# Sums of the u half moved to GpSimd, scores of five tiles in four quarters of the array, and a new order of steps

## The chip, the cores and the metric

The program runs on one core of a Trainium2 chip. A core has TensorE (PE, with its weight loads as PEld), VectorE (DVE), ScalarE (ACT), GpSimd (POOL) and SyncE (SP), which issues all transfers here. Each engine takes its instructions strictly in the order in which the program lists them, and waits on semaphores. The metric is device microseconds of one execution; the median of three runs is compared.

## The reference, cut to what matters

```python
def _attn_ref(q, k, v):            # 8 batches, 8 heads, 576 tokens, head_dim 64
    q_c, k_c, v_c = (a.reshape(B, H, 9, 64, 64) for a in (q, k, v))   # chunks of 64 tokens
    scores = np.matmul(q_c, k_c.transpose(0, 1, 2, 4, 3)) / np.sqrt(D)
    attn = softmax(scores)          # with 1e-9 added to the sum
    return np.matmul(attn, v_c).reshape(B, H, S, D)

def _moe_ref(x, w_in, g_ln, w_sg, b_sg, w_out):   # x: (8, 576, 512)
    h = gelu_tanh(x @ w_in)                       # w_in: 512 x 1024
    u, v = h[..., :512], h[..., 512:]
    v_n = layer_norm(v) * g_ln                    # eps 1e-6
    v_s = einsum('ts,bsd->btd', w_sg, v_n) + b_sg[None, :, None]
    return x + (u * v_s) @ w_out
```

The host hands w_in and w_out over as pairs of 32-bit words of double precision numbers; the kernel makes a high and a low part of each value of them.

## The kernel before

**Tiling.** The 4608 tokens are 36 tiles of 128. A step is named by a letter and a number. For tile t, A loads q, k, v, S makes scores and softmax (L484, L505), T the transposed weights (L544), O the product with v and the split of x into a high part xh, a low part xl and the plain xf (L571, L607). Tiles from 5 on that come in pairs have P and Q in the place of S and O. For batch b, v is the v half (v_unit, L645: product, gelu, layer norm), u the u half (u_unit, L696, or by seven partial products, q), s the product over tokens (L721) and o or p the output product.

**Weights.** W and w make the high and low words of w_in's v half in four pieces, X and x those of its u half (L278 to L283). The begin step loads nothing; it works on a landed piece: ACT takes the absolute value of the upper word (L186), DVE rebuilds the float f and two half-width remainders p and q (L188 to L233). The end step (pair_end, L235) lets ACT write the high word hi = -f, rounded, and lets TensorE add four terms in PSUM, f by a float32 identity, q and p by two bfloat16 multiples of the identity, and hi by the rounded identity (L246). ACT copies the sum out as the low word (L248).

**Partial products.** From batch 2 on the u half and the output product use sums of quarters of the weights, a scheme with seven products in the place of eight. The sums of w_in's quarters are the steps E0 to E3 (sum_product, L360): TensorE adds 4, 2, 2 and 4 quarters by identities in PSUM (L370), ACT and DVE split the sum into high and low (L375 to L380), and SP stores it to DRAM, from where a ring of four buffers is filled later (begin_ring, L384). The sums for w_out are made on GpSimd already (sum_step, L321 to L334). The steps Y turn w_out into high and low words, in eight pieces (o_w, L285).

**Scores.** An array of 128 by 128 can be used as four quarters of 64 by 64. From tile 5 on, each head and chunk is placed by the function half (L456) so that all four quarters occur (L502). Tiles 0 to 4 use only the two quarters on the diagonal, rows 0 to 63 with columns 0 to 63, and rows 64 to 127 with columns 64 to 127 (L493).

**Order.** The order of work is written out by hand: ORDER (L53 to L108) is a string of 1641 step names, and each occurrence runs the named step's generator up to its next yield. Every engine's queue is this order. In PSUM, three two-bank buffers (pm) go round among the products, and two banks (banks) serve the attention.

## Time and profile before

| what | value |
|---|---|
| median of 3 runs | 502.53 us (502.31 to 502.89) |
| profiled execution | 501.2 us |
| its span | 499.4 us |
| TensorE busy | 480.9 us, 96% of the span |
| VectorE, ScalarE, GpSimd busy | 393.1, 339.0, 118.4 us |
| mean granted TensorE clock | 1.00 |

The span runs from the first to the last instruction of the core; 1.8 us of the profiled execution lie around it, and the execution is 1.3 us below the median of the runs. Busy time of TensorE comes from matmul records with modelled ends, so the pace of a series is read from one start to the next, not from the mean duration. A releaser behind an arrow names what ended an engine's idle time. Times of a stretch are microseconds from the span's start.

### The profile page before, as it was taken

The numbers are of one execution on the slowest core, as the hardware profiler recorded it, in microseconds if no ns is written. First come the engines' busy times: TensorE is split into PE (matmuls) and PEld (weight loads), VectorE is DVE, ScalarE is ACT, GpSimd is POOL, SyncE is SP. The second block draws the span as 40 slices with busy tenths as digits, with TensorE's granted clock in tenths as the row PEclk, the third lists the DMA queues.
The fourth block names the chain that finished last, engine by engine and source line by source line (L and its number), as shares of the span: only waits on it lengthen the run. The fifth ranks groups of instructions, "written<-read, shape, count | busy, mean of one in ns | idle before, by whom it ended". The sixth has DMA issues, their size and how long they took to land.

```text
span 499.4 us, 12551 instructions
## 1 busy us (share of the span) xinstructions
PE 480.9 (96%) x5107; PEld 440.6 (88%) x5112; DVE 393.1 (79%) x678; ACT 339.0 (68%) x643; POOL 118.4 (24%) x106
## 2 busy tenths in 40 slices
PE   4899999999999999999999999999999999999996
PEld 2567799889999899997999889997999889998996
DVE  8887969896844797878859788778959788868666
ACT  5787898844655779849894588638885597724420
POOL 0112100010291432116210261114320271105200
PEclk9999999999999999999999999999999999999999
DMA  7976301269276883887887938297876936093616
GB/s 290 368 206 201 111 22 45 86 169 310 74 217 231 281 265 112 226 282 198 270 216 209 298 106 276 62 296 228 250 211 201 297 112 210 6 308 116 226 41 214
DMA packets 70189, 97.98 MB, mean 196 GB/s; under 512 B 36978, under 2 KB 50290, under 8 KB 70132
## 3 DMA queue, kind: packets, MB, share of 16 engines
q1 hardware_dynamic: 70132, 97.18, 62.5%
q8 instruction: 40, 0.66, 0.6%
q14 instruction: 17, 0.14, 0.1%
HBM read 80.38 MB, written 16.78 MB: 195 GB/s over the span
## 4 chain that ended last, share of the span: by engine, by line
PE 79%; ACT 8%; DVE 8%; DMA 3%; issue 1%; SPq 0%; ACTq 0%; DVEq 0%
PE pm L731 23%; PE pm L654 14%; PE pm L852 12%; PE pm L784 11%; PE pm L910 5%; PE pm L703 5%; PE banks L502 3%; PE pm L601 3%; DMA wsg<-w_in 2%; ACT ptT L566 2%; PE pm L246 2%; ACT hs L658 1%; DMA qkv_t<-qkv 1%; ACT L658 1%; DVE blocks L556 1%
## 5 line engine op out<-in xcount | busy, mean ns | idle before, releaser
L731 PE MATMUL pm<-wsg,v 128*128 128x288 f32 x768 | 108.1, 296 | 0.7 <-DVE u L796 0.7
L731 PEld LDWEIGHTS pm<-wsg,v 128*128 128x128 f32 x768 | 103.8, 189 | 1.5 <-DVE u L796 1.0
L667 POOL TENSOR_TENSOR sm<-sm,neg_half 128x1 f32<-128x1 f32 x36 | 28.4, 791 | 126.2 <-DVE sm L665 120.0
L539 POOL TENSOR_TENSOR pt<-pt,den 128x1024 f32<-128x1024 f32 (+1 forms) x15 | 26.4, 1760 | 131.8 <-DVE den L536 123.9
L654 PE MATMUL pm<-wv_h,xl 128*128 128x512 f32 x128 | 51.8, 404 | 2.4 <-ACT xf L633 1.3
L566 ACT COPY ptT<-blocks 32x256 f32<-32x256 f32 x124 | 50.1, 404 | 2.3
L654 PE MATMUL pm<-wv_h,xh 128*128 128x512 f32 x128 | 50.6, 395 | 0.0
L654 PE MATMUL pm<-wv_l,xh 128*128 128x512 f32 x128 | 50.6, 395 | 0.0
L784 PE MATMUL pm<-xt,ring 128*128 128x288 f32 x288 | 42.8, 297 | 0.0
L852 PE MATMUL pm<-gh,ring 128*128 128x288 f32 x192 | 40.9, 297 | 0.0
L784 PEld LDWEIGHTS pm<-xt,ring 128*128 128x128 f32 x288 | 39.5, 188 | 0.8
L662 DVE BATCH_NORM_STATS2 sm<-hs 128x6 f32<-128x512 f32 x36 | 24.8, 688 | 19.3 <-ACT hs L658 19.2
L737 DVE TENSOR_TENSOR u<-pm,u 128x576 f32<-128x576 f32 x24 | 18.0, 752 | 19.2 <-PE pm L731 17.1
L784 PE MATMUL pm<-xh,ring 128*128 128x288 f32 x144 | 32.0, 298 | 0.3 <-ACT hs L658 0.3
L654 PEld LDWEIGHTS pm<-wv_h,xl 128*128 128x128 f32 x128 | 24.0, 188 | 8.8 <-ACT xf L633 2.2
L852 PEld LDWEIGHTS pm<-gh,ring 128*128 128x128 f32 x192 | 31.5, 188 | 0.3
L852 PE MATMUL pm<-tv,ring 128*128 128x288 f32 x216 | 31.7, 296 | 0.0
L675 ACT ACTIVATE v<-hs,sm 128x512 fp32r<-128x512 f32 x32 | 22.9, 721 | 12.3 <-DVE hs L669 12.1
L852 PEld LDWEIGHTS pm<-tv,ring 128*128 128x128 f32 x216 | 29.9, 188 | 0.6
L669 DVE SCALAR_TENSOR_TENSOR hs<-hs,sm,g_bc 128x512 f32<-128x512 f32 x36 | 29.6, 828 | 0.0
L654 PEld LDWEIGHTS pm<-wv_h,xh 128*128 128x128 f32 x128 | 24.0, 188 | 5.8
L852 PE MATMUL pm<-gl,ring 128*128 128x288 f32 x96 | 28.3, 295 | 0.0
(175 smaller groups left out, 1144.9 us busy)
## 6 DMA issues: line engine op xcount, KB each, us to landing
ring<-factors SPq DMA_DIRECT2D x84, 512.0 KB, 4.3
qkv_t<-qkv SPq DMA_DIRECT2D x32, 512.0 KB, 5.0
qkv_t<-qkv SPq DMA_DIRECT2D x124, 64.0 KB, 4.0
out_dram<-u SPq DMA_DIRECT2D x18, 288.0 KB, 5.3
factors<-fac SPq DMA_DIRECT2D x16, 256.0 KB, 2.8
out_dram<-ot SPq DMA_DIRECT2D x14, 288.0 KB, 2.1
qkv_t<-qkv SPq DMA_DIRECT2D x3, 768.0 KB, 11.7
wsg<-w_in SPq DMA_DIRECT2D x4, 512.0 KB, 4.1
```

The lines of the kernel that those rows point to most:

```text
L539: eng.tensor_tensor(pt, pt, den.unsqueeze(2).broadcast_to([P, n, D]), op=ALU.mult)
L566: nc.scalar.copy(ptT[q[1 - a], :, a, :], blocks[q[a], :, 1 - a, :])
L654: nc.tensor.matmul(pv, a[:, kt, tok], c[:, kt, :], start=(i == 0), stop=(i == 11))
L662: nc.vector.bn_stats(st, h)
L667: nc.gpsimd.tensor_tensor(rs, rs, neg_half, op=ALU.pow)
L669: nc.vector.scalar_tensor_tensor(h, h, mv[:, 0:1], g_bc, op0=ALU.subtract, op1=ALU.mult)
L675: nc.scalar.mul(hi, h, rs)
L703: nc.tensor.matmul(pm[:, j, :HS], a[:, kt, dc], c[:, kt, j * HS : (j + 1) * HS], start=(i == 0), stop=(i == 11))
L731: nc.tensor.matmul(pm[:, j, :HS], a[:, dc], c[:, m, j * HS : (j + 1) * HS], start=(i == 0), stop=(i == len(ops) - 1))
L784: nc.tensor.matmul(pm[:, e, :HS], a[:, k, e * P : (e + 1) * P], c[:, k, :], start=starts and i == 0, stop=i == len(ops) - 1, skip_group_ch ...
L852: nc.tensor.matmul(pm[:, e, :HS], a[:, k, e * P : (e + 1) * P], c[:, k, :], start=starts and i == 0, stop=i == len(ops) - 1, skip_group_ch ...
L910: nc.tensor.matmul(pm[:, j, :HS], a[:, kt, ec], c[:, kt, j * HS : (j + 1) * HS], start=(i == 0), stop=(i == len(ops) - 1),)
```

## The change

Four things change. In the end step of the four u pieces, GpSimd adds f and hi into a bfloat16 remainder d, and TensorE adds three bfloat16 terms in the place of four. The quarter sums E0 to E3 are ten GpSimd additions in the order of sum_inner, in a buffer that shares its place with w_out's high words, in the place of twelve matmuls; ACT and DVE split the sums from SBUF, not from PSUM. The first five tiles' scores lie in four quarters and two PSUM banks, with the softmax and the product with v indexed to match. ORDER is written anew; of its 61 lines one stands below.

```diff
@@ -51,61 +51,61 @@
 ORDER = """
-L0 L1 A0 L2 M0 L3 A1 W0 A2 A3 W0 A4 W0 W1 W0 W1 w0 W0 W1 W0 W1 S0 W1 w1 W1 W2 w0 S0 W2 S0
...
+L0 L1 A0 L3 M0 L2 A1 W0 A2 A3 W0 A4 W0 W1 W0 W1 w0 W0 W1 W0 W1 S0 W1 w1 W1 W3 w0 S0 W3 S0
...
@@ -116,6 +116,7 @@
 X_LOW_ON = {5: "vector", 6: "vector", 7: "vector", 4: "vector"}
 U_KEPT_ON_ACT = (1, 5, 6)
 RING = 4
+REST_ON_POOL = {"u": (0, 1, 2, 3), "v": ()}
 
 
 ON_POOL = ("l0", "l1")
@@ -232,15 +233,21 @@
         yield
         nc.vector.scalar_tensor_tensor(q, lw, 9, top, op0=ALU.logical_shift_right, op1=ALU.bitwise_or)
 
-    def pair_end(n, hi, lo, st):
+    def pair_end(n, hi, lo, st, rest=False):
 
         f = st[:, 2 * n : 3 * n].bitcast(F32)
         p, q = st[:, 3 * n : 4 * n].bitcast(BF16)[:, 1::2], st[:, : 2 * n].bitcast(BF16)[:, :n]
         shape = lambda a: a.rearrange("p (k c) -> p k c", k=hi.shape[1]) if len(hi.shape) == 3 else a
         nc.scalar.mul(hi, shape(f), -1.0)
         yield
+        if rest:
+
+            d = st[:, : 2 * n].bitcast(BF16)[:, n : 2 * n]
+            nc.gpsimd.tensor_tensor(shape(d), shape(f), hi.bitcast(F32), op=ALU.add)
+            yield
         ps = ps_m.tile([P, 2, 512], F32, name="pm")[:, 0, :n]
-        terms = [(ident, f), (low[0], q), (low[1], p), (ident_r, hi)]
+        ones = ident_r.bitcast(BF16)[:, 1::2]
+        terms = [(low[0], q), (low[1], p), (ones, d)] if rest else [(ident, f), (low[0], q), (low[1], p), (ident_r, hi)]
         for i, (a, c) in enumerate(terms):
             out_ps = shape(ps) if c is hi else ps
             nc.tensor.matmul(out_ps, a, c, start=(i == 0), stop=(i == len(terms) - 1))
@@ -261,7 +268,7 @@
         yield from pair_begin(DH, staged["v", kt])
 
     def v_w_end(kt):
-        yield from pair_end(DH, wv_h[:, kt, :], wv_l[:, kt, :], staged["v", kt])
+        yield from pair_end(DH, wv_h[:, kt, :], wv_l[:, kt, :], staged["v", kt], kt in REST_ON_POOL["v"])
         yield
         u_w_load(kt)
 
@@ -280,7 +287,7 @@
 
     def u_w_end(dt):
         cols = slice(dt * P, (dt + 1) * P)
-        yield from pair_end(DH, wu_h[:, :, cols], wu_l[:, :, cols], staged["u", dt])
+        yield from pair_end(DH, wu_h[:, :, cols], wu_l[:, :, cols], staged["u", dt], dt in REST_ON_POOL["u"])
 
     def o_w(et, half):
         nonlocal wout_h, wout_l
@@ -353,31 +360,28 @@
         yield
         keep_factor("o", p, (hi, lo))
 
-    def begin_sums():
-        held["neg"] = const.tile([P, P], F32R, name="neg", tag="low")
-        nc.scalar.mul(held["neg"], ident, -1.0)
-
-    def sum_product(n):
-
-
-        h11, l11, h12, l12, h21, l21, h22, l22 = quarters("u")
-        if n in (0, 3):
-            held["sum"] = ps_m.tile([P, 2, 512], F32, name="pm")
-        ps = held["sum"][:, 0].rearrange("p (k e) -> p k e", k=2)
-        pos, neg = (((h21, l21, h22, l22), ()), ((), (h11, l11)), ((), (h12, l12)), ((h11, l11), (h21, l21)))[n]
-        terms = [(ident_r, a) for a in pos] + [(held["neg"], a) for a in neg]
-        for i, (a, c) in enumerate(terms):
-            nc.tensor.matmul(
-                ps, a, c, start=n in (0, 3) and i == 0, stop=i == len(terms) - 1, skip_group_check=n in (1, 2)
-            )
-        yield
+    def sum_inner(n):
+
+
+        if n == 0:
+            t = w_out_tile(0, F32)
+            held["sums"] = [t[:, i * 4 * P : (i + 1) * 4 * P].rearrange("p (k e) -> p k e", k=2) for i in range(3)]
+        h11, l11, h12, l12, h21, l21, h22, l22 = (a.bitcast(F32) for a in quarters("u"))
+        a, c, d = held["sums"]
+        steps = (
+            ((a, h21, h22, ALU.add), (c, l21, l22, ALU.add), (a, a, c, ALU.add)),
+            ((a, a, h11, ALU.subtract), (a, a, l11, ALU.subtract)),
+            ((d, h12, a, ALU.subtract), (d, d, l12, ALU.add)),
+            ((c, h11, h21, ALU.subtract), (d, l11, l21, ALU.subtract), (c, c, d, ALU.add)),
+        )[n]
+        for k, (o, x, y, op) in enumerate(steps):
+            nc.gpsimd.tensor_tensor(o, x, y, op=op)
+            yield
+        src = steps[-1][0]
         hi, lo = factor_tiles()
-        nc.scalar.mul(hi, ps, -1.0 if n == 2 else 1.0)
-        yield
-        if n == 2:
-            nc.vector.scalar_tensor_tensor(lo, ps, -1.0, hi.bitcast(F32), op0=ALU.mult, op1=ALU.subtract)
-        else:
-            nc.vector.tensor_tensor(lo, ps, hi.bitcast(F32), op=ALU.subtract)
+        nc.scalar.copy(hi, src)
+        yield
+        nc.vector.tensor_tensor(lo, src, hi.bitcast(F32), op=ALU.subtract)
         yield
         keep_factor("u", (5, 6, 3, 7)[n], (hi, lo))
 
@@ -457,7 +461,7 @@
 
 
         m = t % NINE
-        j = (h + (c if m == 4 else (m - (m > 4)) % 2)) % 2
+        j = (h + (c if m == 4 or t < PE_TILES else (m - (m > 4)) % 2)) % 2
         return slice(j * D, (j + 1) * D)
 
     def att_load(t):
@@ -486,11 +490,12 @@
         if tiles[0] < PE_TILES:
             for t in tiles:
                 qt = state[t]
-                sc = ps_m.tile([P, 2, H, D], F32, name="pm")[:, 0]
+                pm = ps_m.tile([P, 2, 512], F32, name="pm")
+                sc = pm[:, :, : HP * D].rearrange("p j (hp s) -> p j hp s", hp=HP)
                 for h in range(H):
                     for c in range(2):
-                        r = slice(c * D, (c + 1) * D)
-                        nc.tensor.matmul(sc[r, h, :], qt[r, 0, h, :], qt[r, 1, h, :], start=True, stop=True)
+                        r, o = slice(c * D, (c + 1) * D), half(t, h, c)
+                        nc.tensor.matmul(sc[o, h % 2, h // 2, :], qt[r, 0, h, :], qt[r, 1, h, :], start=True, stop=True)
                 yield from softmax((t,), sc)
             return
         for i, t in enumerate(tiles):
@@ -510,8 +515,9 @@
         pt = att.tile([P, (2 if big else 1) * H, D], F32, name="pt", tag="pt2" if big else "pt1", bufs=1)[:, :n]
         nmax = small.tile([P, 2 * H], F32, name="nmax", bufs=2)[:, :n]
         den = small.tile([P, 2 * H], F32, name="den", bufs=1)[:, :n]
-        rows = (lambda a: a) if t < PE_TILES else (lambda a: a.rearrange("p (c k) s -> p c k s", c=2))
-        cols = (lambda a: a) if t < PE_TILES else (lambda a: a.rearrange("p (c k) -> p c k", c=2))
+        order = "(k c)" if t < PE_TILES else "(c k)"
+        rows = lambda a: a.rearrange(f"p {order} s -> p c k s", c=2)
+        cols = lambda a: a.rearrange(f"p {order} -> p c k", c=2)
         yield
         nc.vector.tensor_reduce(cols(nmax), sc, axis=AX.X, op=ALU.max, negate=True)
         scale = 1.0 / math.sqrt(D)
@@ -522,7 +528,7 @@
             yield
             for h in range(H):
                 col = slice(h, h + 1)
-                src = sc[:, h, :] if t < PE_TILES else sc[:, h // HP, h % HP, :]
+                src = sc[:, h % 2, h // 2, :] if t < PE_TILES else sc[:, h // HP, h % HP, :]
                 nc.scalar.activation(pt[:, h, :], src, AF.Exp, bias=nmax[:, col], scale=scale, accum_out=den[:, col])
         else:
             yield
@@ -578,10 +584,9 @@
             for hp in range(HP):
                 for c in range(2):
                     for j in range(2):
-                        r = slice(j * D, (j + 1) * D)
+                        r, q = slice(j * D, (j + 1) * D), half(t, j, c)
                         nc.tensor.matmul(
-                            xo[r, hp, c * D : (c + 1) * D], vt[r, c, hp, :], ptT[r, hp, c * D : (c + 1) * D],
-                            start=True, stop=True,
+                            xo[r, hp, c * D : (c + 1) * D], vt[r, c, hp, :], ptT[r, hp, q], start=True, stop=True
                         )
             yield from keep(t, xo.rearrange("p hp (c s) -> p c hp s", c=2))
             return
@@ -936,7 +941,7 @@
         "Y": lambda k: o_w(k // 2, k % 2), "R": lambda k: begin_ring(), "f": lambda k: load_factor(),
     }
     steps.update({
-        "B": sum_step, "C": split_sum, "K": lambda k: keep_quarters("o"), "N": lambda k: begin_sums(), "E": sum_product,
+        "B": sum_step, "C": split_sum, "K": lambda k: keep_quarters("o"), "E": sum_inner,
         "k": lambda k: keep_quarters("u"),
     })
```

The order of the engines shows this at three places. First TensorE around the first v_unit (v00): `pm<-wv_h,xl` is its first matmul, `wsg_189` is the first u piece, `banks<-ptT,qkv_t` an O step and `banks<-ident,pt` a T step. Before:

```order
L493 MATMUL pm<-qkv_t 64x64 x16
L246 MATMUL pm<-wsg_189,ident 128x512
L246 LDWEIGHTS low
L246 MATMUL pm<-wsg_189,low 128x512
L246 LDWEIGHTS low
L246 MATMUL pm<-wsg_189,low 128x512
L246 MATMUL pm<-wu,ident 128x512
L582 MATMUL banks<-ptT,qkv_t 64x64 x16
L549 MATMUL banks<-ident,pt 128x128 x4
L654 MATMUL pm<-wv_h,xl 128x512
```

After, from the last matmuls of that v_unit on:

```order
L659 MATMUL pm<-wv_l,xh 128x512
L659 MATMUL pm<-wv_h,xh 128x512
L253 LDWEIGHTS low
L253 MATMUL pm<-wsg_189,low 128x512
L253 LDWEIGHTS low
L253 MATMUL pm<-wsg_189,low 128x512
L253 LDWEIGHTS ident
L253 MATMUL pm<-wsg_189,ident 128x512
L588 MATMUL banks<-ptT,qkv_u 64x64 x16
L555 MATMUL banks<-ident,pt 128x128 x4
```

The end of the first u piece stood two steps ahead of v00 and now stands right behind it, with three bfloat16 matmuls in the place of four terms, and ahead of tile 3's O step, whose data lie in `qkv_u`.

Second GpSimd from its first tile work on: `xl<-xf,xh` is the low part of x of tiles 0 and 1, `sm<-sm,neg_half` the layer norm's inverse root, `sums` the w_out sums, `wu` w_in's u half. Before:

```order
L626 TENSOR_TENSOR xl<-xf,xh 128x2x4x64 x2
L414 MEMSET wsg_550 64x576
L667 TENSOR_TENSOR sm<-sm,neg_half 128x1 x9
L539 TENSOR_TENSOR pt<-pt,den 128x1024 x2
L334 TENSOR_TENSOR sums<-wout_981 128x512
```

After (`wsg_189` to `wout_439` are the four u pieces, `wout_667` the buffer of the sums):

```order
L631 TENSOR_TENSOR xl<-xf,xh 128x2x4x64
L246 TENSOR_TENSOR wsg_189<-wsg_189,wu 128x512
L631 TENSOR_TENSOR xl<-xf,xh 128x2x4x64
L246 TENSOR_TENSOR wsg_203<-wsg_203,wu 128x512
L672 TENSOR_TENSOR sm<-sm,neg_half 128x1
L246 TENSOR_TENSOR wout_314<-wout_314,wu 128x512
L418 MEMSET wsg_604 64x576
L672 TENSOR_TENSOR sm<-sm,neg_half 128x1
L378 TENSOR_TENSOR wout_667<-wu 128x512
L246 TENSOR_TENSOR wout_439<-wout_439,wu 128x512
```

The pieces' additions and the sums of E0 now stand between the low parts of x and the inverse roots, where nothing stood.

Third ScalarE ahead of the Q step of tiles 7 and 8, in the s units of batch 0: `pt<-pt` is the exponential of those tiles, `ptT<-blocks` their transposed weights, `st` a piece of w_out, `gh<-gt` the gated value. Before:

```order
L531 ACTIVATE pt<-pt 128x1024
L199 ACTIVATE st<-st 128x256
L186 ACTIVATE st<-st 128x256
L747 CAST gh<-gt 128x576
L199 ACTIVATE st<-st 128x256
L633 COPY xf<-pm 128x2x4x128
L186 ACTIVATE st<-st 128x256
L560 COPY ptT<-blocks 128x512
L566 COPY ptT<-blocks 32x8x32 x4
```

After:

```order
L537 ACTIVATE pt<-pt 128x1024
L382 CAST fac<-wout_667 128x512
L638 COPY xf<-pm 128x2x4x128
L382 CAST fac<-wout_667 128x512
L200 ACTIVATE st<-st 128x256
L187 ACTIVATE st<-st 128x256
L752 CAST gh<-gt 128x576
L200 ACTIVATE st<-st 128x256
L187 ACTIVATE st<-st 128x256
L566 COPY ptT<-blocks 128x512
L572 COPY ptT<-blocks 32x8x32 x4
```

Two copies of quarter sums (`fac<-wout_667`) stand ahead of the transposed weights, and the high word of a w_out piece has gone behind them.

## Rows read from the trace of the kernel before

**Rows 1.** The page, part 1: engines' busy us, share of span, instructions.
```profile
PE 480.9 (96%) x5107; PEld 440.6 (88%) x5112; DVE 393.1 (79%) x678; ACT 339.0 (68%) x643; POOL 118.4 (24%) x106
```

**Rows 2.** Windows: stretch, length, then PE, PEld, DVE, ACT, POOL busy; clock; DMA.
```profile
30.00:90.00 60.00, 58.19 (x650) 50.31 (x652) 50.52 (x95) 51.72 (x106) 6.65 (x7) 1.00 0.36 109
40.00:120.00 80.00, 80.00 (x805) 72.15 (x806) 68.13 (x146) 61.60 (x113) 7.62 (x10) 1.00 0.43 125
70.00:80.00 10.00, 10.00 (x188) 9.77 (x188) 8.14 (x12) 9.83 (x16) 0.00 (x0) 1.00 0.20 54
80.00:90.00 10.00, 10.00 (x128) 9.58 (x127) 9.90 (x23) 8.49 (x19) 0.00 (x0) 1.00 0.09 28
110.00:120.00 10.00, 10.00 (x129) 9.64 (x128) 6.87 (x12) 4.63 (x7) 0.55 (x1) 1.00 0.96 265
180.00:200.00 20.00, 19.27 (x254) 18.57 (x253) 17.16 (x25) 19.27 (x30) 6.03 (x5) 1.00 0.47 157
```

**Rows 3.** Chain that ended last, in order of time: start, us, what.
```profile
12.06 10.83 DMA wsg<-w_in
...
70.65 1.09 PE banks L502 x64
...
109.86 0.92 PE pm L370 x4
```

**Rows 4.** Timeline of PE: start, us, line, tiles, count, idle before it.
```profile
14.54 1.15 PE L493 MATMUL pm<-qkv_t 64*64 64x64 f32 x32 [0.61 <-DMA qkv_t<-qkv]
...
32.66 0.48 PE L654 MATMUL pm<-wv_h,xl 128*128 128x512 f32 x1
...
36.84 0.66 PE L549 MATMUL banks<-ident,pt 128*128 128x128 f32 x4 [1.14 <-DVE xl L631]
38.17 1.15 PE L582 MATMUL banks<-ptT,qkv_u 64*64 64x64 f32 x32 [0.68 <-ACT xf L633]
```

**Rows 5.** Timeline of PE, the end steps of the last two u pieces.
```profile
54.92 1.12 PE L246 MATMUL pm<-wout,ident 128*128 128x512 f32 x2
55.88 0.38 PE L246 MATMUL pm<-wout,low 128*128 128x512 bf16 x1
56.13 0.59 PE L246 MATMUL pm<-wu,ident 128*128 128x512 f32 x1
56.56 1.02 PE L246 MATMUL pm<-wout,ident 128*128 128x512 f32 x2
```

**Rows 6.** Timelines of POOL and DVE around the low parts of x.
```profile
19.82 1.27 POOL L626 TENSOR_TENSOR xl<-xf,xh 128x512 fp32r<-128x512 f32 x1 [18.53 <-ACT xh L624]
30.68 1.29 POOL L626 TENSOR_TENSOR xl<-xf,xh 128x512 fp32r<-128x512 f32 x1 [9.59 <-ACT xh L624]
...
19.96 1.69 DVE L539 TENSOR_TENSOR pt<-pt,den 128x512 f32<-128x512 f32 x1
...
22.28 0.17 DVE L521 TENSOR_SCALAR nmax<-nmax 128x8 f32<-128x8 f32 x1
...
26.43 0.69 DVE L539 TENSOR_TENSOR pt<-pt,den 128x512 f32<-128x512 f32 x1
...
30.76 1.25 DVE L521 TENSOR_SCALAR nmax<-nmax 128x8 f32<-128x8 f32 x1
```

**Rows 7.** Groups by line, shapes apart: POOL's sums, DVE's subtractions and ACT's copies beside them.
```profile
L334 POOL TENSOR_TENSOR sums<-wout 128x512 f32<-128x512 f32 x4 | 5.6, 1418 | 0.0
...
L352 DVE TENSOR_TENSOR fac<-sums,fac 128x512 fp32r<-128x512 f32 x4 | 2.7, 687 | 0.7 <-DMA out_dram<-ot 0.6
...
L350 ACT CAST fac<-sums 128x512 fp32r<-128x512 f32 x4 | 2.4, 622 | 0.3 <-DVE den L536 0.2
```

**Rows 8.** Timelines of ACT and PE where tiles 7 and 8 meet.
```profile
84.92 1.65 ACT L566 COPY ptT<-blocks 32x256 f32<-32x256 f32 x4
...
87.71 1.16 PE L601 MATMUL pm<-ptT,qkv_t 64*64 64x64 f32 x64
```

More of the change, by code (lines that the diff above doesn't have):

```diff
@@ new lines @@
+W3 S0 W3 W3 w1 W3 w0 w0 S0 W2 S0 w3 W2 T0 W2 w1 w1 W2 S1 T0 W2 w2 O0 S1 W2 S2 A5 O0 S1 w2
+O0 S2 S1 O0 S2 O0 S1 S3 w2 w2 S1 O0 D8 S1 X0 S3 S2 X0 T1 X0 X0 S4 S3 T1 X0 S2 S3 O1 S2 x0
+X0 T2 A6 O1 S3 x0 X1 w3 S4 T2 S3 O1 S3 O2 X2 O1 S4 X1 w3 w3 T3 A7 O2 v00 X2 S4 O2 X2 X1 X2
+X1 T3 x0 X2 O2 S4 x1 X2 O3 S4 G0 X1 T4 X1 v00 O3 v01 v00 x1 X3 O3 x2 v00 X3 O3 v00 v00 T4 X3 x2
+x0 O4 X3 v01 x1 v00 A8 v02 O4 g0 v01 x1 x3 O4 v00 O4 O4 O4 x2 v01 O4 X3 O4 v01 P5 v01 O4 v02 X3 E0
+v01 u00 v02 x2 v01 g0 x3 v02 g2 P5 g4 v02 v03 g3 g2 g1 g4 v02 g4 g1 g0 x3 v02 g4 v03 x3 v02 v04 k0 P5
@@ new lines @@
+E0 g3 P5 E0 v03 u01 P5 E3 v03 u00 P5 v04 P5 v03 E0 v03 u02 u01 T5 v03 v04 T5 v03 T5 v04 T5 T6 T5 v04 P7
+T5 v04 T6 T6 u03 P7 T6 T6 T6 u02 P7 v04 E0 v04 Q5 v04 v04 E0 E1 v04 v04 s00 Y0 Q5 Y1 E1 u03 Q5 E2 P7
+s01 s00 E2 E1 P7 Q5 E2 E1 P7 Y0 E1 Y0 P7 s00 s02 Y1 Y0 s00 Y1 Y0 T8 Y0 T8 Y1 Y0 Y1 T8 Y0 T8 Y1
+s03 T8 Y0 T8 T7 E2 T7 s02 E2 E3 T7 T7 Y1 T7 T7 E3 s02 s01 Q7 s02 s01 v10 Y1 Y2 Q7 s03 Y3 Y1 s03 Q7
+E3 E3 Q7 v11 s01 E3 Y0 s03 Y2 Y2 Y0 Y1 Y2 Y4 Y2 Y1 v12 Y2 Y5 Y2 v10 Y2 Y3 v10 Y3 v11 Y2 Y3 Y2 v10
@@ new lines @@
+v13 Y3 v12 v10 Y2 Y4 Y3 Y6 v10 Y4 Y5 Y4 Y5 Y3 Y4 v10 Y3 Y4 o00 Y3 Y4 Y3 Y5 Y4 Y5 Y6 Y4 Y6 Y5 Y4
+Y3 v13 Y6 Y7 Y4 Y5 A9 u10 Y6 Y5 Y6 v10 Y6 Y5 Y6 Y5 v11 Y7 Y6 Y7 u11 Y5 u10 Y7 A10 v13 Y6 Y7 Y6 Y7
+v13 Y7 v13 v13 A11 u12 Y7 u11 v12 v13 Y7 v13 Y7 v11 v12 v11 Y7 v11 u13 A12 u12 v12 v12 v11 o00 v12 v11 K0 v12 P9
+u13 s10 P9 o00 P9 P9 s11 P9 s10 P9 s10 P9 s10 P11 s12 T9 P11 T9 T9 s11 T9 T9 T10 T9 s11 P11 T10 s13 s11 T10
+P11 s12 T10 P11 T10 T10 s12 P11 Q9 s13 P11 s12 s13 o01 A13 B0 T12 s13 T12 A14 B1 T12 o02 T12 o01 T12 T11 T12 B5 T11
```

94 lines of the change are left out of this document (39 added, 55 removed).

## The prediction

> **What bounds the kernel now.** I read the page's first part first: TensorE is busy for 96% of the span, VectorE for 79%, ScalarE for 68%, GpSimd for 24% [rows 1]. An average hides stages, so I read the windows next. From 40 to 120 us TensorE shows 80.00 of 80 us, at a granted clock of 1.00 [rows 2]: there, each microsecond of matmul taken out is worth a microsecond, provided that the other engines can follow. Whether they can is the second thing to see in these rows. From 30 to 90 us VectorE works 50.52 of 60 us and ScalarE 51.72 [rows 2]. They have 9.5 and 8.3 us of idle time left; by 110 to 120 us ScalarE is down to 4.63 of 10. Third the chain of work and the timeline of the start. Until about 23 us ScalarE's queue waits for the first piece of w_in's u half: that transfer ends at 12.06 + 10.83 = 22.89 us [rows 3]. The first v_unit begins at 32.66 us, and TensorE then idles twice more, 1.14 and 0.68 us [rows 4].
>
> **The quarter sums** leave TensorE as twelve matmuls. Four of them take 0.92 us on the chain [rows 3], so 0.23 each, and twelve take 2.76 us, all at places where TensorE was never idle. I count 2.76 us in full. ScalarE's copy and VectorE's subtraction for each sum remain, but three of the four now come ahead of the s units' end instead of behind 110 us.
>
> **The low words of the u pieces.** One end step lasts from 54.92 to 56.56, 1.64 us; one bfloat16 matmul in it from 55.88 to 56.13, 0.25 us [rows 5]. Three of these make 0.75 us, so each piece saves 0.89 us of TensorE, and the last three pieces, which lie where TensorE is full, 2.67 us. The first piece moves from ahead of the first v_unit to behind it: 0.75 us enters the full stretch and 1.64 us leaves the start.
>
> **The scores in four quarters.** A tile in two quarters takes 1.15 us [rows 4]; a pair of later tiles in four takes 1.09 [rows 3], so 0.55 for one. Five tiles save 5 x 0.6 = 3.0 us, but all of them ahead of 32.66 us, where TensorE waits for others. I give this no term of its own. The whole that leaves TensorE is 2.76 + 4 x 0.89 + 3.0 = 9.3 us, and that is the upper bound of the gain without new overlap.
>
> **The start.** The same bytes are ordered ahead of the u pieces, so I keep ScalarE's start at about 22.9 us. Behind it the first v_unit needs tile 1's low part, which GpSimd ended at 30.68 + 1.29 = 31.97 us [rows 6], and a free TensorE, which came at 32.66 [rows 4]. The change puts one of two absolute values (0.6 us) behind tile 1's parts and takes 1.64 us out of TensorE's queue ahead of the v_unit. Following both queues piece by piece I get tile 1's low part at about 31.0 and the v_unit at about 31.3, a gain of 1.4 (bounds 0.7, TensorE's own delay alone, and 2.4, if the transfers come a microsecond earlier too). Of the two idle times of 1.82 us behind it the first piece's 0.75 us of work fills a part, and I leave 0.7 us idle, ahead of tile 4's output, whose transposed weights stand behind a table load and other work on ScalarE. That gives 1.4 + (1.82 - 0.7) - 0.75 = 1.8 us.
>
> **Sum without contention:** 2.76 + 2.67 + 1.8 = 7.2 us.
>
> **What is added.** GpSimd gets fourteen additions on tiles of 128x512. Such sums last 1.29 to 1.42 us [rows 6, 7], so 18 to 20 us of GpSimd, in a stretch where it now works 6.65 of 60 us [rows 2]. Its own time is hidden: the quarter sums are not needed until batch 2. What is not hidden is VectorE. While GpSimd made the low part of x at 19.82, VectorE's normalisation of tile 1 took 1.69 us, not the 0.69 of tile 2's; while it made that of tile 1, at 30.68, a tiny scaling took 1.25 us, not 0.17 [rows 6]. So an addition can cost VectorE up to 1.08 us, fourteen up to 15 us. At the other end, VectorE's subtractions beside the w_out sums kept their 687 ns, and it was GpSimd that lasted 1.42 in place of 1.29 [rows 7]; that is a price of nought. No price is below nought, since the removed work was on TensorE and VectorE does the same subtractions. I take 4 us of VectorE time in all, nearer to nought, because half of VectorE's work there reads PSUM or is a reduction. The Trainium skill, page SBUF — State Buffer, section "Who interferes with whom", has a rule that speaks against this change: GpSimd and a VectorE operation with two SBUF inputs exclude each other for a whole instruction. By it all fourteen would block somebody, and if always VectorE, the sum would be a loss; the rows above agree that a wait occurs and show both sides bearing it.
>
> **Whether the cover holds.** The test is the Q step of tiles 7 and 8, which TensorE reaches at 87.71 us; ScalarE ends the transposed weights for it at 84.92 + 1.65 = 86.57 [rows 8]. To come 1.8 + 2.67 = 4.5 us earlier, both helpers must give up idle time. ScalarE has 8.3 us less 1.9 for three early copies of 0.62 [rows 7]; VectorE 9.5 us less 1.4 for two early subtractions of 0.69 [rows 7], less 1.4 that I allow for w_out work moved ahead, less the 4 us above: 2.7 us, plus the 1.1 us that TensorE's weights were early (87.71 less 86.57). That falls short of 4.5 by about 0.6 us, which I take off. In VectorE's queue the waiting subtraction of a quarter sum holds back the softmax and transposes of tiles 7 and 8, and TensorE waits for those. Behind this point ScalarE has room (4.63 of 10 us), and from 180 to 200 us, where ScalarE works 19.27 of 20 us and TensorE 19.27 [rows 2], the last sum's splitting is gone, so I expect neither gain nor loss.
>
> **Forecast:** 7.2 - 0.6 = 6.6 us less. The profiled execution of 501.2 us would become 494.6 and its span 492.8; the median of the runs, 1.3 us above it, goes from 502.5 to **495.9 us**. A difference of about 0.2%, 1 us, is what a measurement here can tell from none.
>
> **The rivals.**
> 1. ScalarE and VectorE cannot follow at all up to the Q step, and only what lies behind it is won: 2.76 us, 499.8 us; with half of the 4.5 us, 497.5. For it: 9.90 and 9.83 of 10 us in the windows before 90 us [rows 2]. Against it: the idle time exists, and the order was written for shorter TensorE steps. Chance of 497.3 to 500.5: 0.22.
> 2. All that is taken out comes through, 9.3 us: 493.2 us. For it: the start is shortened by the scores too, and 0.7 us of idle time left above may vanish. Against it: the transfer that ends at 22.89 us. Chance of 492 to 494.5: 0.15.
> 3. GpSimd's additions make VectorE the bound and the kernel slower. Place: VectorE's queue between the first v_unit and the Q step of tiles 7 and 8. If every addition costs 1.08 us, VectorE loses 15 us, 11 more than counted, and the sum turns to 502.5 - 6.6 + 11 = 507 us. It decides for slower from 10.6 us on, 0.76 us for each of the fourteen. Against it: rows 7, where GpSimd bore the wait. Chance 0.06.
> 4. The change does not do what it says, because TensorE's gain is given back at 180 to 200 us, where ScalarE is full: 502 us, no change. Against it: ScalarE has half its time free from 110 us on and arrives there earlier as well. Chance 0.05.
> The forecast's own case, 494.5 to 497.3, has the rest, 0.52.
>
> **How the numbers follow.** The range leaves out the slower and the unchanged case, 0.11, and some hundredths at either end: 493.0 to 500.0. Faster by over 0.2% is 0.52 + 0.22 + 0.15 = 0.89, within 0.2% is 0.05, slower 0.06.
>
> **What would show it.** The quarter sums' matmuls are gone and u pieces' end steps take about 0.75 us; the first v_unit starts near 31.3 us; the Q step of tiles 7 and 8 near 83.8 us, and with no idle time of TensorE over 1 us in front of it; GpSimd's busy time rises from 118 to about 137 us; VectorE's two-input operations of 0.69 us show up at 1.2 to 1.9 beside GpSimd's additions, with about 4 us more in sum. The forecast is wrong if TensorE idles for microseconds between 40 and 90 us behind VectorE or ScalarE, or if the order opens new waits behind 180 us, where I have followed only the order of TensorE.

## The result, and the profile after

The changed kernel takes 495.75 us (median of six runs, 493.63 to 497.74), the kernel before 501.51 on the same chips (six runs, 499.44 to 502.89). The ratio is 0.9886 with a 95% interval of 0.9849 to 0.9923. The forecast was 495.9, in a range of 493.0 to 500.0. The profiled execution went from 501.2 to 493.63 us, its span from 499.4 to 491.8.

Executions of the changed kernel differ in TensorE's mean granted clock, from 1.00 down to 0.991, and the time goes with it (493.63 and 494.42 us at 1.00; 495.34 to 497.74 at 0.997 and below); the profile shown here is one at 1.00, and so is that of before.

The page's first part and the windows after, to be held against [rows 1] and [rows 2]:

```profile
PE 473.1 (96%) x5087; PEld 434.3 (88%) x5092; DVE 403.5 (82%) x678; ACT 339.3 (69%) x642; POOL 138.1 (28%) x120
```

```profile
30.00:90.00 60.00, 59.03 (x631) 51.20 (x632) 57.75 (x102) 54.30 (x108) 22.55 (x20) 1.00 0.45 142
40.00:120.00 80.00, 79.80 (x813) 73.05 (x813) 75.04 (x148) 60.77 (x110) 23.52 (x22) 1.00 0.50 153
...
180.00:200.00 20.00, 19.79 (x201) 19.29 (x201) 16.37 (x24) 18.75 (x32) 3.47 (x3) 1.00 0.60 170
```

TensorE lost 7.8 us of work, and GpSimd gained 19.7. VectorE, which was busy for 50.52 of the 60 us from 30 to 90, now is for 57.75: 2.25 us of idle time are left. TensorE still has none to speak of from 40 to 120 us.

TensorE's timeline after, at the places of [rows 4], [rows 5] and [rows 8]; then VectorE and GpSimd beside the third u piece; then the chain's transfer, as in [rows 3]:

```profile
30.37 0.50 PE L659 MATMUL pm<-wv_h,xl 128*128 128x512 f32 x1
...
39.22 1.15 PE L588 MATMUL banks<-ptT,qkv_t 64*64 64x64 f32 x32 [0.42 <-ACT ptT L558]
...
43.77 0.61 PE L253 MATMUL pm<-wout,low 128*128 128x512 bf16 x2
44.22 0.38 PE L253 MATMUL pm<-wout,ident 128*128 128x512 bf16 x1
44.53 1.16 PE L507 MATMUL banks<-qkv_t 64*64 64x64 f32 x64
...
82.70 1.16 PE L606 MATMUL pm<-ptT,qkv_t 64*64 64x64 f32 x64
```

```profile
38.95 1.41 POOL L246 TENSOR_TENSOR wout<-wout,wu 128x512 bf16<-128x512 f32 x1
...
38.49 0.75 DVE L674 SCALAR_TENSOR_TENSOR hs<-hs,sm,g_bc 128x512 f32<-128x512 f32 x1
39.15 1.50 DVE L191 TENSOR_SCALAR wout<-wout 128x512 int32<-128x512 int32 x1
```

```profile
11.14 10.28 DMA wsg<-w_in
```

Three things are to be seen. The first v_unit starts 2.29 us earlier (32.66 to 30.37). Of that, 1.47 us lie in the first u piece's transfer, which lands at 21.42 and not 22.89: it is issued 0.92 us earlier (11.14 and not 12.06) and takes 0.55 us less. The u piece's end step takes 0.76 us (43.77 to 44.53; 1.64 before). From the v_unit to the Q step of tiles 7 and 8 it was 55.05 us (32.66 to 87.71) and is 52.33 (30.37 to 82.70). So 5.0 of the 7.6 us are gained by then; the twelve matmuls of the quarter sums, 2.76 us, are the rest, less some tenths.

### The profile page after: what moved, and what is told of

Its sections match the earlier page's. It is cut to its first block, busy times and chain, and to the rows that moved or that the text cites. A ratio compares the mean times of both kernels' runs of the same rounds, so it can differ in the third digit from the quotient of the medians.

```text
span 491.8 us, 12519 instructions
## 1 busy us (share of the span) xinstructions
PE 473.1 (96%) x5087; PEld 434.3 (88%) x5092; DVE 403.5 (82%) x678; ACT 339.3 (69%) x642; POOL 138.1 (28%) x120
## 4 chain that ended last, share of the span: by engine, by line
PE 77%; ACT 9%; DVE 7%; DMA 4%; SPq 1%; issue 1%; ACTq 0%
PE pm L736 23%; PE pm L659 15%; PE pm L857 12%; PE pm L789 11%; PE pm L708 5%; PE pm L915 4%; PE banks L507 3%; PE pm L606 3%; DMA wsg<-w_in 2%; ACT L663 1%; ACT pt L532 1%; ACT ptT L572 1%; DMA qkv_t<-qkv 1%; DVE sm L667 1%; DVE v L682 1%; DMA ring<-factors 1%
## 5 line engine op out<-in xcount | busy, mean ns | idle before, releaser
L566 ACT COPY ptT<-blocks 128x512 f32<-128x512 f32 x31 | 19.0, 619 | 17.9 <-DVE blocks L562 17.7
L682 DVE SCALAR_TENSOR_TENSOR v<-hs,sm,v 128x512 fp32r<-128x512 f32 x32 | 28.1, 884 | 2.6 <-ACT v L680 2.5
```

The lines of the kernel that those rows point to most:

```text
L682: nc.vector.scalar_tensor_tensor(lo, h, rs, hi.bitcast(F32), op0=ALU.mult, op1=ALU.subtract)
```

## Experiments

Each is compared with the kernel before, run on the same chip in the same group. "From the v_unit to the Q step" is the stretch just named: it begins behind the start, and so is hardly touched by what happens there.

**The changed kernel again** (no edit).

> The changed kernel once more, as the reference of this group. Every theory: its time stands to the kernel before as 0.9886 with an interval of about 0.004, as measured first; the profiled span is near 491.8 us, the first piece of the u half lands at about 21.4 us, the first v_unit starts at 30.4 us and the Q step of tiles 7 and 8 at 82.7 us.

Measured: 497.46 us, ratio 0.9904 (0.9872 to 0.9936); the kernel before has a median of 501.12 us in this group. The profile differs from the first mainly in the start; the v_unit comes at 32.85 us, the Q step 52.72 us later. The transfer, the windows of this second profile, and TensorE's timeline:

```profile
11.07 11.87 DMA wsg<-w_in
```


```profile
24.00:26.00 2.00, 0.00 (x0) 0.00 (x0) 1.93 (x5) 2.00 (x15) 0.00 (x0) 1.00 1.19 215
26.00:28.00 2.00, 1.46 (x34) 1.40 (x35) 1.93 (x6) 1.53 (x4) 0.00 (x0) 0.89 0.42 127
28.00:30.00 2.00, 2.00 (x6) 1.01 (x5) 1.93 (x5) 1.23 (x3) 1.26 (x1) 0.50 0.61 143
30.00:32.00 2.00, 2.00 (x25) 1.13 (x25) 1.24 (x4) 2.00 (x4) 1.01 (x1) 0.76 0.73 219
```

```profile
26.54 1.15 PE L588 MATMUL banks<-ptT,qkv_t 64*64 64x64 f32 x32 [2.74 <-ACT ptT L558]
...
28.52 1.91 PE L253 MATMUL pm<-wout,ident 128*128 128x512 f32 x2
30.23 0.97 PE L253 MATMUL pm<-wout,low 128*128 128x512 bf16 x2
...
32.85 0.48 PE L659 MATMUL pm<-wv_h,xl 128*128 128x512 f32 x1
...
85.57 1.16 PE L606 MATMUL pm<-ptT,qkv_t 64*64 64x64 f32 x64
```

The granted clock is the column ahead of the last two. The transfer took 11.87 us here instead of 10.28, ScalarE waited for it until 22.96, and TensorE idled 2.74 us ahead of tile 1's output. Behind that idle time the granted clock is 0.50, the lower of the two levels (1.2 of 2.4 GHz), and the next end step's first two matmuls take 1.71 us from start to start of what follows, not 0.86. The v_unit is 2.5 us late against the first profile: 1.5 us of that are there when tile 1's output starts (26.54 against 25.05), 1.0 comes with the fall. Of twelve executions of the changed kernel in both groups nine have a mean granted clock under 0.998; they take 495.34 to 498.09 us, the other three 493.63 to 494.42. The kernel before has such executions too: 23 of the 75 whose clock is on record lie under 0.998, with a median of 502.89 us against 500.96 of the other 52. No profile of the kernel before caught one, so where its clock falls stays open.

**Scores of tiles 0 to 4 on the diagonal again**, and **four quarters for tile 0 alone**. In the function half:

```diff
+        if t < PE_TILES:              # second kernel: if 1 <= t < PE_TILES:
+            return slice(c * D, (c + 1) * D)
```

> The changed kernel with the scores of tiles 0 to 4 on the diagonal quarters again, all else the same. Theory: tile 0's scores run at the start, where TensorE goes at half its later pace, and the end step of the first v piece queues behind them; its buffer is what the transfer of the first u piece waits for. So the scores take 1.9 us and not 1.06, that transfer is issued at about 12.0 us (11.14 in the changed kernel), lands near 22.4, the first v_unit starts near 31.3 us (30.37), the Q step of tiles 7 and 8 near 83.6 (82.70), and the whole is 0.9 us slower: a ratio of 0.990 to the kernel before. Rival, the prediction's own view: TensorE waits for others in that stretch, so shorter scores are worth nothing; the v_unit stays at 30.4 us and the ratio at 0.9886.

> The changed kernel with four quarters for tile 0's scores alone; tiles 1 to 4 lie on the diagonal. Theory (tile 0 delays the transfer): the first u piece lands at 21.4 us and the first v_unit starts at 30.4 to 30.7 us, as with all five in four quarters; the ratio is within 0.001 of the changed kernel's. Rival (each of the five tiles' 0.5 to 0.6 us counts, because TensorE's queue ahead of the v_unit bounds its start): the v_unit starts 1 us or more later than 30.4.

Measured: 495.45 us, ratio 0.9870 (0.9846 to 0.9894), and 495.42 us, 0.9872 (0.9847 to 0.9896). The chain's transfer and TensorE's rows with all five on the diagonal:

```profile
12.03 10.55 DMA wsg<-w_in
...
7.12 1.98 PE L500 MATMUL pm<-qkv_t 64*64 64x64 f32 x32 [7.12 <-DMA qkv_t<-qkv]
...
31.58 0.50 PE L661 MATMUL pm<-wv_h,xl 128*128 128x512 f32 x1 [0.22 <-POOL xl L633]
```

The v_unit with tile 0 alone in four quarters:

```profile
30.64 0.50 PE L661 MATMUL pm<-wv_h,xl 128*128 128x512 f32 x1
```

With tile 0 alone in four quarters the transfer is issued at 11.19 us and the v_unit starts at 30.64, with all five at 11.14 and 30.37, with none at 12.03 and 31.58. So the mechanism holds up to the issue: tile 0's scores delay the first end step, that step the buffer, the buffer the issue of the transfer, by 0.8 to 0.9 us each. That the landing follows is not shown. In the eleven profiles on record in which the issue lies at 10.98 to 11.19 us, ScalarE starts on the piece at 21.35 to 22.96 us; in the two with the old scores of tile 0 (issue at 12.03 and 12.06) at 22.61 and 22.92. The time that I expected does not come: the two kernels here differ in tile 0's scores alone, both keep their clock, and their medians are 0.03 us apart. All twelve executions of these two kernels have a mean clock of 0.998 or more, and both are 2.0 us faster than the changed kernel in the same group. Longer scores of tiles 1 to 4 leave TensorE less idle ahead of tile 1's output (1.15 and 0.23 us in the two profiles).

**One filler step longer.** Both kernels have a step D8 there, eight float32 matmuls on the identity that nobody reads.

```diff
-O0 S2 S1 O0 S2 O0 S1 S3 w2 w2 S1 O0 D8 S1 X0 ...
+O0 S2 S1 O0 S2 O0 S1 S3 w2 w2 S1 O0 D12 S1 X0 ...
```

> The changed kernel with one number of its order changed: the step D8, eight float32 matmuls on the identity whose result nobody reads and which stand in both kernels between tile 3's scores and tile 1's transposes, is D12. It waits for nothing in that stretch, other than the matmuls of the run a_keep, which were held by ScalarE's copy and started behind the idle time. Four more take 1.0 us; tile 1's transposes come 1.0 us later (about 23.4 us), still ahead of ScalarE's copy of them at 24.3. Theory (the clock falls where TensorE idles 2.5 us or more ahead of tile 1's output product, which happens when the first u piece lands late): the idle time is 0.5 to 2 us now, the mean granted clock is 0.998 or more in nearly every execution, as in the kernels with longer scores, and the median is 494 to 495 us, ratio 0.985 to 0.988, with no execution over 496.5. Rival (the falls do not depend on that idle time, and the kernels with longer scores escaped them for another reason): clock under 0.998 in most executions, ratio 0.990.

Measured: 495.35 us (494.14 to 496.13), ratio 0.9875 (0.9851 to 0.9899); mean clock 0.998 or more in all six executions. In the profile the transfer landed late again (ScalarE started on it at 22.55 us), and:

```profile
20.39 2.94 PE L933 MATMUL pm<-ident 128*128 128x128 f32 x24
...
25.63 0.69 PE L498 MATMUL pm<-qkv_t 64*64 64x64 f32 x32 [1.86 <-ACT pt L532]
```

```profile
26.00:28.00 2.00, 2.00 (x61) 1.80 (x52) 1.97 (x5) 1.23 (x4) 0.34 (x1) 1.00 0.23 70
```

The idle time is 1.86 us, the clock stays at 1.00, and the v_unit starts at 31.52 us; the median is 0.35 us above the range that I gave. So 0 of 18 executions with more work in that place that waits for nothing have the low clock, against 9 of 12 without. The profiles of all kernels in the new order agree: the clock falls behind idle times of 2.31 to 2.84 us in that place (five profiles, the shortest with the old end step below) and stays up behind 0.23 to 1.86 (six). The length alone does not say it, though: ahead of 15.34 us in the changed kernel's second profile TensorE idled 2.58 us, and the clock stayed at 1.00. That tile 4's scores now wait for ScalarE's exponentials, which they did not with D8, I did not expect and did not settle.

**A filler in the wrong place**, and **a filler at the very start**: a step d of matmuls on the identity into the attention's own banks, five ahead of O1's first occurrence, or ten ahead of S0's.

```diff
+    def keep_pace(n):
+        for _ in range(n):
+            nc.tensor.matmul(banks[:, 0, :P], ident, ident, start=True, stop=True)
```

> The changed kernel with one step more: five float32 matmuls of 128x128 on the identity (about 1.3 us of TensorE at its later pace), whose result nobody reads, between tile 4's scores and tile 1's output product, where TensorE waits for ScalarE and with it for the first u piece. Theory (in most executions the transfer lands late, TensorE idles 2.5 to 3 us there, and its granted clock then falls to 0.50 for some 4 us, as in the changed kernel's second profile at 26 to 31 us; where it idles 1.5 us, as in the first, the clock stays 1.00): with the idle time under 2 us the clock stays up in nearly all executions, the mean granted clock is 0.998 or more in each, and the median comes to 494 to 495 us, ratio 0.986 to 0.988. Rival (the falls have another cause, or the added matmuls delay tile 1's output): the clock falls as often as before, three executions in four, and the ratio stays at 0.990.

> The changed kernel with ten such matmuls at the very start, ahead of tile 0's scores, from about 2.4 us to 7 us, where TensorE has nothing to do. Theory: TensorE's first 4 us of work run at half of the later pace whatever the work is (the end step of the first v piece took 2.9 us there and 1.64 later), so with the matmuls in front the scores take 0.55 us and not 1.06, the end step about 1.7 us, and the transfer of the first u piece is issued at about 9.6 us and not 11.1; it lands up to 1.5 us earlier, the first v_unit starts at 29 to 30 us and TensorE idles less at 23 to 25 us. Time 492.5 to 494 us, ratio 0.983 to 0.986. Rival (the transfer lands when the queue ahead of it is empty, not by its own start): the v_unit stays at 30.4 us or later and the ratio at 0.988 to 0.990.

Measured: 498.14 us, ratio 0.9930 (0.9906 to 0.9955), and 494.98 us, 0.9872 (0.9847 to 0.9898). Of the first kernel TensorE's rows, of the second TensorE's, SyncE's and a window:

```profile
26.25 2.50 PE L942 MATMUL banks<-ident 128*128 128x128 f32 x10 [2.82 <-ACT ptT L562]
28.68 1.97 PE L592 MATMUL banks<-ptT,qkv_t 64*64 64x64 f32 x32
```

```profile
2.37 4.63 PE L942 MATMUL banks<-ident 128*128 128x128 f32 x20 [2.37 <-ACT ident L158]
7.21 1.13 PE L502 MATMUL pm<-qkv_t 64*64 64x64 f32 x32 [0.20 <-DMA qkv_t<-qkv]
8.27 1.12 PE L257 MATMUL pm<-wsg,ident 128*128 128x512 f32 x2
...
9.91 1.02 PE L257 MATMUL pm<-wsg,ident 128*128 128x512 f32 x2
...
15.23 1.09 PE L559 MATMUL banks<-ident,pt 128*128 128x128 f32 x4 [3.63 <-DVE pt L549]
```

```profile
9.92 2.08 SPq L287 DMA_DIRECT2D wsg<-w_in  x2
```

```profile
16.00:20.00 4.00, 4.00 (x100) 3.34 (x99) 3.52 (x6) 2.17 (x4) 0.00 (x0) 0.69 1.01 399
```

The five matmuls (two records each) waited for ScalarE's copy out of the other bank, so they stood behind the idle time and not in it, and took 2.4 us of the profile at the low clock. Six of the eight executions have a mean clock under 0.998. The run says nothing on my theory, and its ratio is not told from the changed kernel's (0.9904, overlapping intervals). The ten at the start do what they were for: the first end step takes 1.64 us from its first start to the next step's (8.27 to 9.91; 3.02 and 2.66 in the changed kernel's two profiles), and the transfer is issued at 9.92 us. But ScalarE gets it at 22.82, no earlier; the rival was right there, and the v_unit starts at 31.80. TensorE then idles 3.63 us from 11.6, and its granted clock is 0.69 from 16 to 20 us. That costs little, since TensorE waits again at 24 to 26 us: the six executions lie between 494.49 and 495.82 us although their mean clocks are 0.992 to 0.997.

**The old end step of the u pieces.**

```diff
         if rest:
-            d = st[:, : 2 * n].bitcast(BF16)[:, n : 2 * n]
-            nc.gpsimd.tensor_tensor(shape(d), shape(f), hi.bitcast(F32), op=ALU.add)
             yield
-        terms = [(low[0], q), (low[1], p), (ones, d)] if rest else [(ident, f), (low[0], q), (low[1], p), (ident_r, hi)]
+        terms = [(ident, f), (low[0], q), (low[1], p), (ident_r, hi)]
```

> The changed kernel with the old end step of the u pieces: no addition on GpSimd, four terms on TensorE, in the same places of the order. Theory (TensorE is the bound from the first v_unit on): 4 x 0.89 = 3.6 us later at the Q step of tiles 7 and 8, which starts at 86.3 us, and as much at the end; ratio 0.9957. Rival (VectorE or ScalarE sets the pace up to that step): TensorE's idle time swallows part of it and VectorE gains the 1.8 us by which its work was lengthened beside the four additions; the Q step starts before 84.7 us and the ratio is under 0.993.

Measured: 497.75 us, ratio 0.9936 (0.9912 to 0.9959). The idle time and the clock ahead of the v_unit, and the two ends of the stretch:

```profile
25.81 1.65 PE L584 MATMUL banks<-ptT,qkv_t 64*64 64x64 f32 x32 [2.31 <-ACT ptT L554]
...
32.10 0.48 PE L655 MATMUL pm<-wv_h,xl 128*128 128x512 f32 x1
...
87.15 1.24 PE L602 MATMUL pm<-ptT,qkv_t 64*64 64x64 f32 x64
```

```profile
26.00:28.00 2.00, 2.00 (x35) 1.88 (x33) 2.00 (x4) 0.81 (x2) 0.00 (x0) 0.56 0.31 91
```

From the v_unit to the Q step it is 55.05 us: 2.72 more than in the changed kernel's first profile, 2.33 more than in its second, which has a clock fall ahead of the v_unit as this one has. The theory had 3.56 and the rival less than 2. At a mean clock of 0.998 or more the five executions have a median of 496.8 us, 2.4 over the changed kernel's 494.4 (the median of its three such executions). So TensorE sets the pace for the larger part, and two thirds to three quarters of its removed work comes through, net of what the four additions cost VectorE.

**The quarter sums on TensorE again**, first with the fourth sum in batch 2 as before the change, then with all four in batch 1. sum_inner is replaced by the old begin_sums and sum_product; in ORDER the E steps go to their old places, N0 behind x3. Second kernel, one place:

```diff
-... v22 O13 v20 O13 z25 v21 E3 O13 P14 ...
+... P11 s12 s13 o01 E3 A13 B0 T12 s13 T12 E3 A14 ...
```

> The changed kernel with the quarter sums E0 to E3 as twelve matmuls again, at the places that they had before the change; scores, u pieces and the rest of the order stay new. Theory: the twelve matmuls cost their 2.76 us on a full TensorE, three sums in batch 1 and one in batch 2, the Q step of tiles 7 and 8 stays at 82.7 us within 0.3, and the ratio to the kernel before is 0.994. Rival (the ten additions on GpSimd cost VectorE time that TensorE pays): without them the stretch up to the Q step gets shorter by 1 us or more, and the ratio stays under 0.992.

> The changed kernel with the quarter sums as twelve matmuls, all four sums in batch 1 this time: the earlier such kernel had the fourth in batch 2 and showed idle times of TensorE of 2.1 and 2.7 us there, at 177 and 189 us, that neither other kernel has. Theory (the sums are worth their matmuls, 2.76 us, and the rest of the 4.9 us came from the fourth sum's place): no idle time of over 1.5 us at 170 to 195 us, and 2.5 to 3.5 us slower than the changed kernel between executions of the same granted clock: 497 us at clock 1.00 against 494.2, ratio near 0.995 to 0.997. Rival (sums on TensorE cost 5 us wherever the fourth stands, through the PSUM buffer that they hold or through ScalarE and VectorE): 499 us at clock 1.00, ratio about 1.00.

Measured: 502.31 us, ratio 1.0007 (0.9983 to 1.0031), and 499.79 us, 0.9973 (0.9956 to 0.9990). The two ends of the stretch from the v_unit to the Q step, in the first kernel and in the second:

```profile
33.64 0.48 PE L666 MATMUL pm<-wv_h,xl 128*128 128x512 f32 x1
...
86.38 1.16 PE L613 MATMUL pm<-ptT,qkv_t 64*64 64x64 f32 x64
```

```profile
31.00 0.50 PE L666 MATMUL pm<-wv_h,xl 128*128 128x512 f32 x1 [0.37 <-POOL xl L638]
...
83.11 1.16 PE L613 MATMUL pm<-ptT,qkv_t 64*64 64x64 f32 x64
```

Without the ten additions, the first kernel's stretch takes 52.74 us; that of the changed kernel's second profile, with a clock fall ahead of it as here, takes 52.72. Without a fall it is 52.11 in the second kernel and 52.33 in the changed kernel's first profile. So beside these ten additions TensorE loses 0.2 us at most. The first kernel's rest is in part in waits that my placing made; TensorE's rows of the first kernel, then of the second:

```profile
179.58 0.40 PE L796 MATMUL pm<-xh,ring 128*128 128x288 f32 x1 [1.90 <-DVE fac L391]
191.39 2.20 PE L796 MATMUL pm<-xt,ring 128*128 128x288 f32 x12 [2.51 <-DMA ring<-factors]
```

```profile
135.98 0.62 PE L381 MATMUL pm<-wu,neg 128*128 128x512 f32 x2
138.01 0.53 PE L922 MATMUL pm<-gh,wout 128*128 128x288 f32 x2 [1.41 <-DVE fac L391]
```

At a clock of 0.998 or more the second kernel has a median of 499.35 us, 5.0 over the changed kernel; 2.76 us are the matmuls, 1.4 is this wait for VectorE's split of the sum, 0.4 is there at the Q step of the profile (83.11 against 82.70), and some tenths are left over. That is the rival's 499 us, with a wait of the kind that it named; the ratio lies at the upper end of the theory's. The kernel before has the matmuls without such a wait. So 2.76 us as the worth of the sums in an order made for them is argued from the rows and was not measured alone; in this order they cost 5.0.

**Parts in the old order**: the scores alone, then scores and remainders. half, att_scores, softmax and att_out as after the change; then pair_end too, and in ORDER one occurrence more of each x step:

```diff
-x0 T2 X0 A6 S3 O1 S4 ...
+x0 x0 T2 X0 A6 S3 O1 S4 ...
```

> The kernel before with one part of the change alone: scores of tiles 0 to 4 in four quarters, old order. Theory (tile 0's scores hold up the transfer of the first u piece): it lands about 0.9 us earlier than 22.89, the first v_unit starts near 31.8 us and not at 32.66, and the whole is about 0.9 us faster: ratio 0.998. Rival (the prediction's view, no term): start and time unchanged, ratio 1.000.

> The kernel before with two parts, the scores and GpSimd's remainder for the u pieces, in the old order (one more step name for each piece, right behind its first). Theory (the gains are TensorE's and add up): 0.9 + 4 x 0.89 = 4.5 us faster than before less what the first piece loses ahead of the first v_unit, where TensorE waits anyway: 3.6 to 4.5 us, ratio 0.991 to 0.993; the new order then is worth less than 1 us. Rival (the order is needed, since the piece's end step on TensorE now waits for an addition of 1.3 us that the old order leaves no time for): idle times of TensorE of about 1 us ahead of the end steps, and a ratio over 0.994.

Measured: 500.00 us, ratio 0.9980 (0.9961 to 0.9998), and 503.92 us, 1.0047 (1.0027 to 1.0066). With the scores alone the transfer is issued at 11.19 us and the v_unit starts at 31.53, 1.13 earlier, as the theory had it. Two of the twelve executions have a mean clock under 0.998, against 11 of 29 of the kernel before on that chip: in the old order the shorter scores do not bring the falls. With the remainders as well TensorE waits, as the rival had it:

```profile
29.61 0.39 PE L257 MATMUL pm<-wsg,low 128*128 128x512 bf16 x1 [1.12 <-DVE wsg L238]
33.08 0.66 PE L562 MATMUL banks<-ident,pt 128*128 128x128 f32 x4 [1.56 <-DVE pt L552]
...
59.05 0.60 PE L257 MATMUL pm<-wout,low 128*128 128x512 bf16 x2 [1.59 <-ACT hs L670]
```

From the v_unit to the Q step it takes 58.0 us, 2.95 more than before the change although TensorE has 2.7 us less to do there. The releasers are VectorE and ScalarE, not GpSimd, so the rival's cause, the addition that comes too late, is not what these rows show. The granted clock falls as well (0.50 at 40 to 42 us, 0.57 at 60 to 64), and all twelve executions have a mean clock under 0.998; how much of the 2.95 us that is stays open.

**Every new addition twice.**

```diff
             nc.gpsimd.tensor_tensor(o, x, y, op=op)
+            nc.gpsimd.tensor_tensor(o, x, y, op=op)
```

(and the same in pair_end)

> The changed kernel with each of the fourteen new additions on GpSimd issued twice in a row (the second of some changes the value, so the sums are other numbers; the time is what counts). It doubles what VectorE suffers beside them: operations lengthened by some 4.8 us in the changed kernel, 8 to 10 us here. Theory (VectorE has idle time left): the Q step of tiles 7 and 8 moves by less than 0.5 us from 82.7 and the ratio by less than 0.001. Rival (the prediction's account, by which the cover was used up and each microsecond more on VectorE is one on TensorE): the Q step starts 3 to 5 us later and the ratio is 0.995 to 0.998.

Measured: 508.44 us, ratio 1.0123 (1.0091 to 1.0156). The Q step starts at 95.46 us, 62.73 behind the v_unit: 10.0 us more than in the changed kernel's second profile. The window and two rows of it:

```profile
30.00:90.00 60.00, 53.46 (x566) 45.77 (x569) 55.69 (x76) 45.07 (x91) 38.40 (x30) 1.00 0.42 129
```

```profile
95.46 0.48 PE L608 MATMUL pm<-ptT,qkv_t 64*64 64x64 f32 x4 [3.86 <-ACT ptT L574]
...
87.91 0.62 ACT L384 CAST fac<-wout 128x512 fp32r<-128x512 f32 x1 [4.03 <-POOL wout L380]
```

My theory of idle time left is dead. But the run mixes two costs. Taking each VectorE operation beside the new additions against the shortest of its line and shape, the excess rises from 5.1 us in the changed kernel to 15.3. And GpSimd itself is late: ScalarE waits 4.03 us for a sum, and behind that copy in ScalarE's queue stand the transposed weights of tiles 7 and 8, held by VectorE for another 0.98 us, for which TensorE then waits 3.86 us. Four idle times of TensorE make up 8.8 of the 10 us, all ended by ScalarE (1.20, 2.02, 1.76 and 3.86). How the 10 us divide between the two costs is open.

## Why the prediction was right, and where its steps were not

The total is right to 0.2 us, and part of that is luck. The forecast starts from 502.5 us, the median of three executions of the kernel before; six in the group of the result have 501.51. So a gain of 6.6 us was forecast and 5.76 was measured, and in the second group it is 3.7 (501.12 to 497.46). Between executions with a mean clock of 0.998 or more it is 6.6 us (500.96, the median of 52, to 494.38, that of three). The working is right in size for those; late transfers and falls of the clock, which it did not have, take a part back in most executions, and a starting value 1 us too high made up for that.

- **The start** was forecast to give 1.8 us, 1.4 of it at the v_unit. In the changed kernel's first profile the v_unit is 2.29 us earlier, with a transfer of 10.28 us; in its second, with 11.87, it is 0.19 us later; with the sums on TensorE and the clock up it starts at 31.00 us, 1.66 earlier. So 1.4 lies inside a spread that it did not foresee. The step that was too simple is "I give this no term of its own" for the scores. I asked whether TensorE waits there, and it does; I did not ask what waits for TensorE. The issue of a transfer did, through a buffer: tile 0's scores alone move it by 0.8 to 0.9 us. Whether that is worth time is open: nothing in the new order (495.45 and 495.42 us), about 0.2% for all five tiles in the old one (0.9961 to 0.9998). That the transfer could come a microsecond earlier stood in the prediction as a bound, with no cause.
- **The clock** was not in the prediction at all. I read the granted clock of 1.00 in the windows of one execution as a property of the kernel. In the new order shorter scores make TensorE's idle time ahead of tile 1's output longer; when the transfer is late as well, the clock goes to its lower level. In the second profile the v_unit is 2.5 us late, 1.5 by the transfer and 1.0 by the clock. The Trainium skill, page TensorE: Matmul & The Clock Gate, section "What's actually happening", says that the clock is halved after idleness and comes back with sustained work; the second profile of the changed kernel agrees (0.50 at 28 to 30 us, behind 2.74 us of idleness). In three of twelve executions the kernel takes 494.1 us on average, 1.8 under the forecast; in the others up to 498.1.
- **The u pieces**, 0.89 us each and 2.67 us for three, were priced a quarter to a third too high: from the v_unit to the Q step the old end step costs 2.33 to 2.72 us for four pieces, 0.58 to 0.68 each. The removed terms took what the rows said; the new end steps take 0.7 to 1.0 us in the changed kernel, not 0.75, which explains about 0.1 us each. The rest is not settled. The stretch as a whole came out nearer: the forecast's terms for it (1.12 - 0.75 + 2.67 - 0.6) give 2.4 us, and it is 2.72 and 2.33 shorter in the two profiles.
- **The sums**, 2.76 us: right as far as the comparison of the two profiles goes (7.6 us in all, 5.0 of them by the Q step, leave 2.6); not measured alone.
- **VectorE beside GpSimd**, 4 us of lengthened operations and 0.6 us of them paid by TensorE: 5.1 us in the trace, by the excess over the shortest of each line and shape. A scaling or a two-input operation of VectorE on SBUF that starts during an addition is mostly longer (1.50 us at 39.15 us, with 0.43 elsewhere); reductions, statistics and operations with an input in PSUM grow by 0.04 us at most. An addition that starts during such an operation lasts longer itself: 1.41 us at 38.95, where VectorE had begun at 38.49, and up to 1.75, not 1.29. The Trainium skill, page SBUF — State Buffer, section "Who interferes with whom", says that issue order decides who blocks, and these rows agree. What TensorE pays for it came out smaller: without ten of the fourteen additions the stretch is not shorter, or shorter by 0.2 us (52.74 and 52.72 us, 52.11 and 52.33).
- **The cover** was judged rightly as nearly used up: 2.25 us of VectorE's idle time are left from 30 to 90 us, and twice the additions cost 10 us. Rival 3, which priced 11 us more on VectorE at 507 us, has its mechanism there: 508.44 us with 15.3 us of excess, though GpSimd's own lateness is in that too.
- **The order** had no term of its own. It should have had: scores and remainders in the old order give 503.92 us, those two in the new order, sums still on TensorE, 499.79 or 502.31 by the place of the fourth sum. The same parts are a loss of 0.5%, a gain of 0.3% or neither (1.0047, 0.9973, 1.0007) by the order alone, waits and falls of the clock included.
- **Behind 180 us** neither gain nor loss was expected. A group of 84 matmuls of the s units starts at 310.0 us before and 302.1 after, 7.9 us earlier; at the end it is 7.6.

## What to carry to other kernels

Where an engine waits, its work is still not free of a price: look for the transfer or buffer that waits for that work, check whether an earlier issue also lands earlier, and look for the clock that the engine's idleness may bring down. When the start hangs on a transfer whose time varies, price a change from more than one execution of both kernels, and read the granted clock of each: three executions of the kernel before put the start of this forecast 1 us too high. When additions go to GpSimd, count the idle time that VectorE has left in that stretch, and the queue behind each copy that waits for a sum: here 7 of VectorE's 9.5 us were used up without a loss to be seen on TensorE, and twice the additions cost 10 us.
